# One chunk's band attention moves from TensorE to VectorE, idle products fill TensorE's gaps, and the opening gets a written-out order

## The chip, the cores and the metric

The kernel runs on one core of a Trainium2 chip. The metric is the device time of one execution in microseconds (us); smaller is better.

## What is computed

The reference is attention in two resolutions, added up, and a gated network on the result.

```python
q_d, k_d, v_d = (t.reshape(8, 8, 144, 4, 64).mean(axis=3) for t in (q, k, v))
coarse = softmax(q_d @ k_d.T / 8) @ v_d          # 144 x 144 for each of 8 batches and 8 heads
local = softmax(where(|i - j| < 4, q @ k.T / 8, -1e9)) @ v   # 576 positions, a band of 7
x = repeat(coarse, 4) + local                    # as 4608 tokens of 512
xn = x / sqrt(mean(x * x) + 1e-6) * rms_g
g = xn @ w_gate                                  # 512 x 1536
out = (silu(g) * (xn @ w_val)) @ w_out           # 1536 x 512
```

Inputs of attention are 32-bit floats; the weights come as 64-bit floats and are decoded on the chip into a high and a low fp32r part.

## The kernel before

The 4608 tokens are worked on in 18 chunks of 256. A chunk needs the local attention of its tokens, the coarse attention of the batches that it touches, the norm, and a transposition into `xh` and `xl` (high and low part). Then the class `Forward` runs: `first` (L1259) forms gate and value with 3 products for each of 4 slices of the model dimension, `second` (L1296) multiplies by `w_out` in the same three-product manner. ScalarE does the tanh, VectorE the gating.

The coarse attention of a batch and two heads is a `Coarse`: scores on TensorE (L498), row maxima on VectorE (L507), exponentials on ScalarE (L517), transposes (L526), values (L540). The result goes to DRAM and comes back in the layout of a chunk (`load_up`). For batch 0 the sums over four positions are formed on the chip from raw inputs (`OpeningSums`: one reduction on VectorE for Q and K, L406, and three additions for V, L415); later batches sum in the DMA, with accumulating loads that POOL issues (L356).

The local attention has two forms. `Attention` works on VectorE: a product of Q with a window of seven K rows (L811), a reduction (L815), the softmax, seven products of share and V row, four on ScalarE (L857) and the others on VectorE and POOL (L864), and a reduction (L874), each eight times a chunk. `Early` works on TensorE: scores of 128 tokens against 136 positions with a mask added by a product (L1048, L1050), row maxima (L1063), exponentials (L1074), shares (L1101), transposes (L1108), value products (L1133), with eight small loads a unit for the positions at the unit's edges (L1036), issued by SP, and the coarse part added by a product with a spreading matrix (L1139). Before, chunks 0 and 1 are `Early` (`ON_TENSOR = 2`), the others `Attention`.

The weights come in 20 pieces, by thirds of the network's width. A piece is loaded by SP into one of a few raw buffers (L249), its bits are scaled on ScalarE (L254), extracted on POOL (L264), joined on VectorE (L271), and split into high (ScalarE, L278) and low part (VectorE, L283 and L285). The place of the second third is also that of chunk 0's and 1's raw inputs and band scores, so that it can only be written when these are done with.

What sets the order: up to the planned time of chunk 3 a planner in the kernel's Python, `Plan`, writes each engine's list by hand. A step is a `task` with an engine (or several to choose from), a cost in us, a due time, the tasks that it waits for and the buffers that it takes. At each turn the planner takes the engine that can start first, and on it, of the tasks that could start within 0.15 us of the first, the one with the smallest due. Each engine then runs its list strictly in order. Due times are formulas: `due` for the chunks (48, 107, 158, then 56 apart), `T - 88 + 7 * n` for a chunk's loads and so on. From chunk 3's network on (`FIRST = 3`) a loop emits chunk c's network with the attention of chunk c + 1 between its steps, and the tile scheduler sets the order.

## Time and profile before

| | us |
|---|---|
| median of 3 runs | 1131.25 |
| lowest and highest | 1128.24, 1132.88 |
| the profiled execution | 1137.31 |
| its span, first to last instruction | 1135.5 |

The profiled execution is 6 us longer than the median; 1.8 us of its time lie outside the span. In the profile, PE is TensorE's products, PEld its weight loads, DVE VectorE, ACT ScalarE, POOL GpSimd, and SP the engine that issues most DMAs; SPq, ACTq and POOLq are DMA issues in these queues. A row of the busy time by stage has the stretch in us from the span's start, its length, for each engine the busy time and the number of instructions, the granted clock, the DMA engines' busy share and GB/s. A row of the chain of waits has start, length, and what ran. A row of a group has the line, engine, operation, tiles and shapes, count, then busy us and mean ns, then idle us before the group and what ended it. A line number is that of the kernel before.

### The profile page before, as it was taken

How to read it: one execution, taken by the hardware profiler on the slowest of the kernel's cores; microseconds unless marked ns; L12 is line 12 of the kernel's file. 1: busy time of each engine (PE TensorE's matmuls, PEld its weight loads, DVE VectorE, ACT ScalarE, POOL GpSimd, SP SyncE). 2: the span in 40 equal slices, each digit the busy share in tenths (PEclk: the TensorE clock that was granted, in tenths of full speed). 3: DMA queues.
4: the chain of work that ended last, by engine and by line, in shares of the span. 5: the costliest groups of instructions: out<-in, count | busy, mean ns of one | idle time of the engine just before them, and what ended most of it. 6: DMA issues, size and time to landing. Idle time of an engine off the chain costs nothing.

```text
span 1135.5 us, 21446 instructions
## 1 busy us (share of the span) xinstructions
PE 1083.9 (95%) x7878; PEld 987.3 (87%) x7878; DVE 900.8 (79%) x1519; ACT 597.8 (53%) x2033; POOL 142.2 (13%) x178
## 2 busy tenths in 40 slices
PE   4699969989999999999999999999999999999997
PEld 3567869869999999999999999999999999999997
DVE  5365987869997979797979797979797989887321
ACT  3465547455646555555555555555555473736111
POOL 4242313332111010101010101010000000000000
PEclk9999989989999999999999999999999999999999
DMA  6755644636264344434343435343131313220000
GB/s 161 272 209 142 179 121 110 127 85 151 67 154 91 109 95 120 85 109 94 109 96 105 99 95 109 103 102 98 43 99 43 103 45 101 69 58 19 1 20 19
DMA packets 79619, 114.07 MB, mean 100 GB/s; under 512 B 32666, under 2 KB 41114, under 8 KB 79514
## 3 DMA queue, kind: packets, MB, share of 16 engines
q1 hardware_dynamic: 50026, 89.52, 25.8%
q0 software_dynamic: 10080, 18.59, 10.5%
q10 hardware_dynamic: 19408, 4.60, 1.9%
q8 instruction: 62, 1.02, 0.4%
q14 instruction: 43, 0.35, 0.1%
HBM read 100.86 MB, written 11.80 MB: 99 GB/s over the span
## 4 chain that ended last, share of the span: by engine, by line
PE 88%; DMA 5%; DVE 2%; ACT 2%; SPq 1%; issue 1%; POOL 0%; ACTq 0%; DVEq 0%; POOLq 0%
PE ps_h L1259 50%; PE ps_o L1296 25%; PE ps_a L540 3%; PE ps_a L498 2%; PE ps_a L526 2%; PE ps_a L926 1%; DMA wo<-in_w_val_dram 1%; PE ps_o L1133 1%; SPq L1036 1%; PE ps_h L1050 1%; DMA w<-in_v_pad_dram 1%; DMA w<-in_v_sum_dram 1%; PE ps_a L1133 1%; DMA q_t<-in_q_band_dram 1%; PE ps_a L1108 0%
## 5 line engine op out<-in xcount | busy, mean ns | idle before, releaser
L1259 PE MATMUL ps_h<-xh,w 128*128 128x256 f32 x3456 | 635.5, 281 | 10.7 <-ACT w L278 6.4
L1259 PEld LDWEIGHTS ps_h<-xh,w 128*128 128x128 f32 x3456 | 540.3, 189 | 22.7 <-ACT w L278 6.8
L1259 PE MATMUL ps_h<-xl,w 128*128 128x256 f32 x1728 | 483.5, 280 | 0.0
L1296 PE MATMUL ps_o<-wo,hs 128*128 128x512 f32 x1296 | 333.5, 399 | 1.7 <-POOL hs L1283 1.6
L1259 PEld LDWEIGHTS ps_h<-xl,w 128*128 128x128 f32 x1728 | 327.2, 189 | 6.5 <-issue 1.7
L857 ACT ACTIVATE prod<-kv,sc 128x64 f32<-128x64 f32 x1024 | 263.7, 407 | 30.4 <-DVE sc L848 19.8
L1296 PEld LDWEIGHTS ps_o<-wo,hs 128*128 128x128 f32 x1296 | 233.4, 189 | 46.4 <-POOL hs L1283 2.7
L874 DVE TENSOR_REDUCE x_t<-prod 128x128 f32<-128x896 f32 x128 | 135.0, 1078 | 47.4 <-PE ps_a L926 41.3
L1266 ACT ACTIVATE sil<-ps_h 128x512 f32<-128x512 f32 x108 | 64.5, 597 | 168.3 <-PE ps_h L1259 159.7
L1280 ACT ACTIVATE hs<-sil 128x512 fp32r<-128x512 f32 x108 | 68.2, 631 | 155.0 <-DVE sil L1274 134.2
L811 DVE TENSOR_TENSOR prod<-q_t,kv 128x896 f32<-128x896 f32 x128 | 140.0, 1099 | 0.5
L815 DVE TENSOR_REDUCE sc<-prod 128x14 f32<-128x896 f32 x128 | 136.7, 1076 | 0.5
L1269 DVE SCALAR_TENSOR_TENSOR sil<-sil,ps_h 128x512 f32<-128x512 f32 x108 | 73.5, 681 | 50.1 <-ACT sil L1266 49.8
L864 DVE TENSOR_TENSOR prod<-sc,kv 128x384 f32<-128x384 f32 (+1 forms) x128 | 103.6, 865 | 0.2
L1274 DVE SCALAR_TENSOR_TENSOR sil<-sil,ps_h 128x512 f32<-128x512 f32 x108 | 74.4, 690 | 30.5 <-PE ps_h L1259 30.3
L356 POOL DMA_DIRECT2D qk<-in_qk_sum_dram x42 | 37.7, 899 | 419.1 <-DMA qk<-in_qk_sum_dram 320.2
L1283 DVE TENSOR_TENSOR hs<-sil,hs 128x512 fp32r<-128x512 f32 x100 | 68.7, 687 | 18.9 <-ACT hs L1280 18.7
L897 ACT ACTIVATE up_t<-x_t 128x128 f32<-128x128 f32 x128 | 39.3, 307 | 44.0 <-DVE x_t L887 39.3
L517 ACT ACTIVATE a_g<-ps_a,m_g 72x144 f32<-72x144 f32 x128 | 46.4, 370 | 15.1 <-DVE m_e L1067 8.3
L605 ACT COPY a_g<-ps_a 72x288 f32<-72x288 f32 x63 | 22.8, 400 | 45.5 <-PE ps_a L526 45.3
L356 POOL DMA_DIRECT2D vs<-in_v_sum_dram x42 | 38.5, 916 | 53.3 <-DMA vs<-in_v_sum_dram 46.4
L540 PEld LDWEIGHTS ps_a<-vs,a_g 72*72 72x72 f32 x512 | 41.8, 159 | 1.3 <-ACT w L1074 0.5
(142 smaller groups left out, 806.9 us busy)
## 6 DMA issues: line engine op xcount, KB each, us to landing
kv<-in_k_pad_dram SPq DMA_DIRECT2D x56, 320.0 KB
kv<-in_v_pad_dram SPq DMA_DIRECT2D x56, 320.0 KB
qk<-in_qk_sum_dram POOLq DMA_DIRECT2D x42, 288.0 KB, 4.5
out_dram<-o_sb SPq DMA_DIRECT2D x96, 72.0 KB
q_t<-in_q_band_dram SPq DMA_DIRECT2D x170, 36.0 KB
vs<-in_v_sum_dram POOLq DMA_DIRECT2D x42, 144.0 KB, 4.4
w<-in_w_gate_dram SPq DMA_DIRECT2D x8, 512.0 KB
w<-in_w_val_dram SPq DMA_DIRECT2D x8, 512.0 KB
```

Of the source, the lines that this page charges most:

```text
L356: nc.gpsimd.dma_start(out=t, in_=(qk_sum, v_sum)[i][self.b, j, :, self.half], accum_op=ALU.add)
L540: nc.tensor.matmul(out=op[:, par, c], lhsT=at[:, kc, c * HALF:(c + 1) * HALF], rhs=self.sums.vs[:, 2 * (self.hp % 2) + par, kc], start=(kc ...
L811: nc.vector.tensor_tensor(out=pr, in0=bcast(q[:, s0:s0 + 2], 2, NO), in1=window(k, s0), op=ALU.mult)
L815: nc.vector.tensor_reduce(out=self.sc[:, j, par, s0:s0 + 2], in_=self.pr[i], axis=AX.X, op=ALU.add,)
L857: nc.scalar.activation(out=self.pr[i][:, o, s], in_=self.v[j, par][:, s0 + s + o], func=AF.Copy, scale=p[:, s, o:o + 1],)
L864: (nc.vector if engine == "DVE" else nc.gpsimd).tensor_tensor(out=self.pr[i][:, a:b], in0=bcast(p[:, :, a:b].rearrange("p s o -> p o s"), ...
L874: nc.vector.tensor_reduce(out=self.x[j][:, s0:s0 + 2, par], in_=pr.rearrange("p o s d -> p s d o"), axis=AX.X, op=ALU.add,)
L1259: nc.tensor.matmul(out=p[n][:, i], lhsT=wi[:, k], rhs=xi[:, k], start=(m == 0), stop=(m == 3 * KT - 1),)
L1269: nc.vector.scalar_tensor_tensor(out=self.sil[n], in0=self.sil[n], scalar=1.0, in1=self.g[n], op0=ALU.add, op1=ALU.mult,)
L1274: nc.vector.scalar_tensor_tensor(out=self.sil[n], in0=self.sil[n], scalar=0.5, in1=self.v[n], op0=ALU.mult, op1=ALU.mult,)
L1283: (nc.gpsimd if engine == "POOL" else nc.vector).tensor_tensor(out=self.hs[n][:, 1], in0=self.sil[n], in1=self.hs[n][:, 0], op=ALU.subtract,)
L1296: nc.tensor.matmul(out=self.o[j], lhsT=lhs[:, cols], rhs=rhs, start=(f == 0 and m == 0), stop=(f == NF - 1 and m == 2),)
```

## The change

Chunk 1 becomes an `Attention`; only chunk 0 stays `Early`. The edge loads of chunk 0's two units go from SP's queue to ScalarE's, as a step of their own. Q's and K's opening sums are three additions instead of one reduction. The planner remembers how long TensorE would idle before a task (`idle`), and `heat` issues products of zeros, 128 wide in contraction and up to 512 columns, into the tile that the next step will overwrite (or, with `fresh=False`, adds zeros to), to fill three quarters of that time where it is over 0.8 us. The small constant loads go from ScalarE's queue to POOL's, behind the start, and the factor matrix `one_sb` is made before the mask. Due times of all 885 tasks are replaced by a list, `RANK`, in tenths of us; among its entries are the edge loads' 126.0 and 104.1 and the small loads' -34.9. Several costs are set anew (score loads of a chunk from 0.15 to 1.8 on SP, exponentials of a `Coarse` from 0.45 to 1.15, transposes from 0.6 to 0.3). The spreading matrix gets smaller, since it serves chunk 0 alone.

```diff
 EDGE = 2 * FAC
-SPREAD = 13 * GRP
+ON_TENSOR = 1
+SPREAD = P * 2 * ON_TENSOR
...
-ON_TENSOR = 2
...
+WARM_AT = 6.5
+WARM_SHARE = 0.75
+WARM_LEAST = 0.6
...
+RANK = [
+    -75, 138, -204, -69, 5, 293, 598, 570, 624, -446, 135, 157, -220, 196, 176, 99, 98, -73, 176, -28, 415,
...
+    -161, 683, -212, 219, 229, -159, 21, 412, 30, 122, 21, 299, -151, 690, -409, 672, 48, 165, 200, 208, 259,
...
+    3289, 1818, 2617, 3401, 3038, 3492, 3243,
+]
...
     def __init__(self, bufs):
-        self.tasks, self.bufs = [], bufs
+        self.tasks, self.bufs, self.idle = [], bufs, 0.0
...
+        if RANK:
+            by = RANK[len(self.tasks)] / 10 - options[0][2]
+            options = [(e, c, d + by) for e, c, d in options]
...
-                        found.append((max(free[e], t.at, at, floor), t))
+                        found.append((max(free[e], t.at, at, floor), t, max(free[e], at)))
...
+            self.idle = s - max(known, WARM_AT) if e == "PE" else 0.0
...
+    zero_sb = const.tile([P, 16], BF16, name="zero_sb")
...
-    X_DUE = [44.0, 60.0]
+    X_DUE = 44.0
...
-    own_place = [(w1[0], QK), (w1[1], QK), (wo[0], 0), (wo[1], 0)]
+    own_place = [(w1[0], QK), (w1[1], QK)]
...
-            add = task("DVE", 2.5, self.add, at, [self.got], allocs=[self.qk_buf])
-            self.q_got = task("ACT", 1.1, self.order, at - 1, [self.got], allocs=[self.q_buf])
+            add = self.got
+            for j in range(1, FAC):
+                add = task(
+                    "DVE", 0.72, lambda j=j: self.add(j), at, [add], allocs=[self.qk_buf] if j == 1 else [], uses=[self.qk_buf],
+                )
+            self.q_got = task("ACT", 1.0, self.order, at - 1, [self.got], allocs=[self.q_buf])
...
-        def add(self):
-            self.qk = glob.tile([P, 2, 2, SD], FP32, name="qk")
-            nc.vector.tensor_reduce(
-                out=self.qk.rearrange("p t h n -> p (t h n)"),
-                in_=self.raw_qk.rearrange("p j x -> p x j"), axis=AX.X, op=ALU.add,
+        def add(self, j):
+            if j == 1:
+                self.qk = glob.tile([P, 2, 2, SD], FP32, name="qk")
+            qk = self.qk.rearrange("p t h n -> p (t h n)")
+            nc.vector.tensor_tensor(
+                out=qk, in0=self.raw_qk[:, 0] if j == 1 else qk, in1=self.raw_qk[:, j], op=ALU.add,
             )
...
+    made = []
+
+    def heat(out, fresh=True):
+
+        n, plan.idle = plan.idle * WARM_SHARE, 0.0
+        cols = 1
+        for d in out.shape[1:]:
+            cols *= d
+        if len(out.shape) > 2:
+            out = out.rearrange({3: "p a b -> p (a b)", 4: "p a b c -> p (a b c)"}[len(out.shape)])
+        cols = min(cols, 4 * P) // P * P
+        for _ in range(int(n * 2400 / cols) if n > WARM_LEAST and made else 0):
+            nc.tensor.matmul(
+                out=out[:, :cols], lhsT=one_sb[:, :out.shape[0]], rhs=bcast(zero_sb, 1, cols // zero_sb.shape[1]), start=fresh, stop=fresh,
+                skip_group_check=not fresh,
             )
...
-                    "ACT", 0.45, lambda par=par: self.powers(par), at, [scale], allocs=[a[par]], uses=[s[par], m, z],
+                    "ACT", 1.15, lambda par=par: self.powers(par), at, [scale], allocs=[a[par]], uses=[s[par], m, z],
...
-                turn = task("PE", 0.6, lambda par=par: self.turn(par), at - TAIL, [exps[par]], allocs=[t[par]], uses=[a[par]])
+                turn = task("PE", 0.3, lambda par=par: self.turn(par), at - TAIL, [exps[par]], allocs=[t[par]], uses=[a[par]])
...
-            values = self.valued = task("PE", 1.3, self.values, at - TAIL, [*copies, *sm.ready_vs], allocs=[o], uses=[*a, sm.vs_buf])
+            values = self.valued = task("PE", 1.15, self.values, at - TAIL, [*copies, *sm.ready_vs], allocs=[o], uses=[*a, sm.vs_buf])
...
+            heat(self.s[0])
...
-                    "SP", 0.15, lambda jp=jp: self.load_score(*jp), T - 88 + 7 * n, allocs=k_bufs[jp],
+                    "SP", 1.8, lambda jp=jp: self.load_score(*jp), T - 88 + 7 * n, allocs=k_bufs[jp],
...
-                    "SP", 0.1, lambda jp=jp: self.load_value(*jp), T - 55 + 7 * n, allocs=[v_bufs[jp]],
+                    "SP", 0.35, lambda jp=jp: self.load_value(*jp), T - 55 + 7 * n, allocs=[v_bufs[jp]],
...
-                load = task("ACT", 0.12, lambda j=j: self.load_up(j), T - 30, up_ready, allocs=[ups[j]], lag=2.5)
+                load = task("ACT", 1.2, lambda j=j: self.load_up(j), T - 30, up_ready, allocs=[ups[j]], lag=2.5)
...
+            heat(tp)
...
-                v_got = task("SP", 0.9, lambda u=u: self.load_values(u), -90 + 12 * u, [clear], uses=[ve], dma=0.5 * MB)
+                v_got = task("SP", 0.4, lambda u=u: self.load_values(u), -90 + 12 * u, dma=0.5 * MB)
+                e_got = task("ACT", 2.8, lambda u=u: self.load_edges(u), -60, [clear], uses=[ve], lag=2.5)
...
-                value = task("PE", 1.75, lambda u=u: self.value(u), at - TAIL, [*parts, v_got], allocs=[y], uses=[*prs, ve])
+                value = task("PE", 2.7, lambda u=u: self.value(u), at - TAIL, [*parts, v_got, e_got], allocs=[y], uses=[*prs, ve])
...
+        def load_edges(self, u):
+            t = HALO + P * u
             first, step = (t - FAC, FAC * (NEAR_K - 1)) if u else (P + HALO, FAC)
             for h in range(H):
                 src = bass.AP(
                     tensor=v_pad.tensor, offset=v_pad.offset + (h * SP + first) * D, ap=[[step * D, 2], [D, FAC], [1, D]],
                 )
-                nc.sync.dma_start(out=self.ve[u][h * EDGE:(h + 1) * EDGE, h * D:(h + 1) * D], in_=src)
+                nc.scalar.dma_start(out=self.ve[u][h * EDGE:(h + 1) * EDGE, h * D:(h + 1) * D], in_=src)
...
+            heat(s)
...
+            heat(y)
...
+            heat(y, fresh=False)
...
-                    lhsT=spread_sb[0][:, GRP + FAC * k:GRP + FAC * k + P], rhs=whole_og["tile"][:, :, :, c],
+                    lhsT=spread_sb[0][:, FAC * k:FAC * k + P], rhs=whole_og["tile"][:, :, :, c],
...
-            if u % 2 == 0:
+            if not hasattr(self, "ss"):
...
+            heat(tp)
...
+                heat(p[n])
...
+            heat(self.o[0], fresh=f == 0)
...
-            "SP", 0.1, lambda: fetch(spot[0].raw_place(spot[1]) if spot else spots[n]), at - 15 - 15 * (fg == 0), allocs=[raw],
+            "SP", 0.35 * m, lambda: fetch(spot[0].raw_place(spot[1]) if spot else spots[n]), at - 15 - 15 * (fg == 0), allocs=[raw],
...
-        bits = task("POOL", (0.93, 1.75)[m - 1], lambda: last_bits("POOL"), at, [got], uses=[raw])
+        bits = task("POOL", (0.75, 1.35)[m - 1], lambda: last_bits("POOL"), at, [got], uses=[raw])
...
-    nc.gpsimd.memset(min_sb, 3e38)
-    for e, at, side in ((0, 0, 0), (1, P - KT, 1), (2, P // 2 - KT, 1), (2, P // 2, 0)):
-        nc.scalar.dma_start(out=min_sb[at:at + KT, e], in_=band_min[(P - KT) * side:(P - KT) * side + KT, side])
-    nc.scalar.dma_start(out=g_sb, in_=rms_g)
-    nc.scalar.dma_start(out=same_sb, in_=same_tok)
+    nc.vector.memset(zero_sb, -1e4)
+    nc.scalar.activation(out=zero_sb, in_=zero_sb, func=AF.Exp)
...
+
+    def make_one():
+        nc.gpsimd.tensor_scalar(out=one_sb, in0=ident_sb, scalar1=2.0 ** 33, scalar2=None, op0=ALU.mult)
+        made.append(one_sb)
...
-        nc.gpsimd.tensor_scalar(out=one_sb, in0=ident_sb, scalar1=2.0 ** 33, scalar2=None, op0=ALU.mult)
...
-        t = first_room(wo[0], A_N + DM, SPREAD)[:HALF]
+        t = first_room(wo[0], 0, SPREAD)[:HALF]
...
-        nc.gpsimd.memset(t, 0.0)
...
-            out=t[:, GRP:GRP + FAC * HALF].rearrange("p (n j) -> p n j", j=FAC), in_=bcast(ident_sb[:HALF, :HALF], 2, FAC),
+            out=t.rearrange("p (n j) -> p n j", j=FAC), in_=bcast(ident_sb[:HALF, :SPREAD // FAC], 2, FAC),
...
+    def load_small():
+        nc.gpsimd.memset(min_sb, 3e38)
+        for e, at, side in ((0, 0, 0), (1, P - KT, 1), (2, P // 2 - KT, 1), (2, P // 2, 0)):
+            nc.gpsimd.dma_start(out=min_sb[at:at + KT, e], in_=band_min[(P - KT) * side:(P - KT) * side + KT, side])
+        nc.gpsimd.dma_start(out=g_sb, in_=rms_g)
+        nc.gpsimd.dma_start(out=same_sb, in_=same_tok)
+
+    small = task("POOL", 6.5, load_small, -40, not_before=2.5, lag=3.0)
+    one_got = task("POOL", 0.6, make_one, -70, not_before=4.5)
...
-        task("POOL", 2.0, make_near, -60, not_before=2.5, allocs=[buf("sil"), buf("sil")]),
+        task("POOL", 1.5, make_near, -60, [one_got], allocs=[buf("sil"), buf("sil")]),
...
-        Early(0).plan(X_DUE[0], (ps_h, "ps_h"), (ps_o, "ps_o")),
-        Early(1).plan(X_DUE[1], (ps_h, "ps_h"), (ps_a, "ps_a")),
+        Early(0).plan(X_DUE, (ps_h, "ps_h"), (ps_o, "ps_o")),
+        Attention(1).plan(),
...
-    atts += [Attention(c).plan() for c in range(ON_TENSOR, FIRST + 1)]
+    atts += [Attention(c).plan() for c in range(2, FIRST + 1)]
...
-    atts[1].turns[0].after += fetched
+    for t in fetched:
+        atts[1].turns[0].after.append(t)
...
```

29 lines of the change are left out of this document (17 added, 12 removed), and 44 rows, old and new, of the table RANK.

## The prediction

> **What bounds the kernel now.** I read the page first, then the busy time by stage, the chain of waits, the queues, and VectorE's groups.
>
> ```profile
> span 1135.5 us, 21446 instructions
> PE 1083.9 (95%) x7878; PEld 987.3 (87%) x7878; DVE 900.8 (79%) x1519; ACT 597.8 (53%) x2033; POOL 142.2 (13%) x178
> ```
>
> TensorE sets the pace of the whole, at 95%. The stages show where the other 5% are. I cut them at the starts of the planned chunks, which the chain of waits gives right below.
>
> ```profile
> core 0: us, PE busy (x) PEld busy (x) DVE busy (x) ACT busy (x) POOL busy (x), PEclk, DMA share, GB/s
> 0.00:8.00 8.00, 0.41 (x1) 0.10 (x1) 1.46 (x1) 1.09 (x1) 6.78 (x22) 1.00 0.78 270
> 8.00:41.00 33.00, 15.81 (x78) 11.74 (x78) 15.55 (x28) 11.74 (x39) 6.37 (x6) 1.00 0.53 139
> 41.00:89.00 48.00, 45.05 (x192) 32.81 (x193) 30.82 (x62) 31.70 (x83) 19.33 (x13) 1.00 0.68 252
> 89.00:110.00 21.00, 19.59 (x70) 14.11 (x69) 10.19 (x15) 9.60 (x27) 5.68 (x6) 1.00 0.59 145
> 110.00:171.00 61.00, 50.62 (x356) 45.67 (x356) 55.05 (x79) 30.85 (x50) 15.84 (x16) 0.92 0.54 146
> 171.00:231.00 60.00, 59.46 (x473) 53.93 (x473) 44.88 (x77) 33.91 (x125) 21.77 (x25) 1.00 0.54 128
> 231.00:252.00 21.00, 15.55 (x82) 11.37 (x81) 13.05 (x24) 11.86 (x47) 8.34 (x19) 0.76 0.28 47
> 252.00:306.00 54.00, 54.00 (x423) 50.47 (x423) 50.06 (x81) 32.95 (x124) 10.81 (x22) 1.00 0.43 104
> 306.00:363.00 57.00, 57.00 (x458) 53.31 (x457) 48.86 (x88) 31.62 (x118) 10.38 (x12) 1.00 0.61 132
> 421.00:1135.00 714.00, 708.44 (x5323) 660.24 (x5321) 579.67 (x982) 369.53 (x1308) 31.63 (x36) 1.00 0.30 78
> ```
>
> ```profile
> 89.75 2.56 PE ps_h L1259 x12
> 92.31 5.61 PE ps_a L1133 x18
> 114.15 2.73 PE ps_h L1259 x24
> 116.88 2.98 PE ps_a L1133 x18
> 145.35 6.86 DMA wo<-in_w_val_dram
> 173.79 1.38 PE ps_h L1259 x12
> 226.81 5.42 DMA up_t<-up
> 251.87 4.11 PE ps_h L1259 x36
> 304.80 7.81 PE ps_h L1259 x67
> ```
>
> The first layer (L1259) of chunk 0 starts at about 89, chunk 1 at about 173, chunk 2 at 252, chunk 3 within the last row, at about 306. From there TensorE is full: 57.00 us of 57, later 708.44 of 714. The diff edits nothing that runs there, so the 1135.5 - 306 = 829.5 us behind it stay, and all that is won or lost is when chunk 3 starts. Three chunks take 54 to 60 us each when they are fed (the stages 252 to 306 and 171 to 231), so of the 306 us some 135 are start-up and waiting: up to 89 no layer runs, about 145 to 158 the weight load of 145.35 and its decoding are waited for, and from 231 to 252 the coarse result that is read back at 226.81.
>
> **The change part by part.** *Edge loads.* What keeps the weights away until 34.8 is SP itself:
>
> ```profile
> 2.35 9.99 SPq L1036 DMA_DIRECT2D kv<-in_v_pad_dram  x8
> 13.73 9.41 SPq L1036 DMA_DIRECT2D kv<-in_v_pad_dram  x8
> 23.69 5.24 SPq L1036 DMA_DIRECT2D kv<-in_v_pad_dram  x8
> 29.48 5.24 SPq L1036 DMA_DIRECT2D kv<-in_v_pad_dram  x8
> 34.77 0.40 SPq L249 DMA_DIRECT2D w<-in_w_gate_dram  x1
> 135.02 0.58 SPq L593 DMA_DIRECT2D kv<-in_k_pad_dram  x1
> 135.65 4.03 SPq L799 DMA_DIRECT2D q_t<-in_q_band_dram  x5
> ```
>
> ```profile
> 41.24 1.12 PE L1108 MATMUL ps_a<-ident_sb,w 128*128 128x128 f32 x4 [10.03 <-ACT a_g L605]
> ```
>
> The 32 small issues hold SP for 9.99 + 9.41 + 5.24 + 5.24 = 29.9 us, with V's sums and every weight behind them; the last row shows TensorE 10.03 us idle until the first weights let ScalarE go on. Sixteen issues vanish with chunk 1's early form, sixteen go to ScalarE's queue. SP gets chunk 1's band loads instead: four score loads at 0.58 + 4.03 = 4.6 us and four value loads at about 0.6, 21 us together, which need not go ahead of the first weights. So these can be issued up to 25 us earlier. Then bytes bind: raw sums (4 MB), a third of the weights (6.3 MB) and chunk 1's bands (3.1 MB), estimated from the shapes, take 50 to 54 us at the 252 to 270 GB/s of the loaded stages. On ScalarE sixteen issues cost from 10 us (16 x 5.24 / 8) to 20 (the 9.99 row, twice); behind them are queued the exponentials of the coarse heads and of chunk 0's band, and TensorE's transposes wait for those. I take 8 of it for the path, nearest to the lower row, as some fall where ScalarE is idle (31.70 busy of 48).
>
> *TensorE.* Chunk 1's early form leaves it: its value products alone are the rows of 18, 5.61 and 2.98 us; with the scores and transposes of two units I put it at 25 us, about three times their sum, half before 89 and half in chunk 0's stretch. The idle products are to quicken the rest: twelve products of L1259 took 2.56 us at 89.75, twenty-four took 2.73 at 114.15, so the opening runs at half speed, though the clock column says 1.00 there. Being busy 45.05 us of 48 did not lift it; some 17 us of wide products behind 89 did. Their cost is nothing in a true gap. If the plan's gaps are not gaps, it is up to three quarters of the 29 us that TensorE idles before 110 (110 - 0.41 - 15.81 - 45.05 - 19.59), 22 us. I take 3, since the queue would mostly wait there for others. By the Trainium skill, "TensorE: Matmul & The Clock Gate", Part 1, some 3.4 us of sustained activity bring the full clock; then it would have come long before 89, the idle products would bring nothing, and the first x would come 10 us later than I say below. The trace disagrees with that, by the 45.05 busy us at half speed.
>
> *First x.* Chunk 0's 89, less 10 for the idle stretch, less 12 for half of chunk 1's early form, less 10 for quicker products (a third of the rest), plus 8 for ScalarE's issues and 3 for idle products: about 68. The bytes allow 54.
>
> *POOL* issues six small loads ahead of the mask that the band scores wait for:
>
> ```profile
> L356 POOL DMA_DIRECT2D qk<-in_qk_sum_dram x42 | 37.7, 899 | 419.1 <-DMA qk<-in_qk_sum_dram 320.2
> ```
>
> At 0.9 us each that is 5.4 us later for the mask, or nothing if the scores wait longer for their raw inputs; 2 of it are in the 68.
>
> *VectorE* is the term that decides.
>
> ```profile
> L811 DVE TENSOR_TENSOR prod<-q_t,kv 128x896 f32<-128x896 f32 x24 | 28.1, 1180 | 0.0
> L815 DVE TENSOR_REDUCE sc<-prod 128x14 f32<-128x896 f32 x24 | 25.8, 1078 | 0.2
> L874 DVE TENSOR_REDUCE x_t<-prod 128x128 f32<-128x896 f32 x20 | 21.7, 1083 | 8.6 <-POOL prod L864 3.5 <-PE ps_a L926 2.4 <-ACT prod L857 2.0
> L874 DVE TENSOR_REDUCE x_t<-prod 128x128 f32<-128x896 f32 x20 | 21.7, 1083 | 8.6 <-POOL prod L864 3.5 <-PE ps_a L926 2.4 <-ACT prod L857 2.0
> L1063 DVE TENSOR_REDUCE m_e<-ps_h 128x2 f32<-128x272 f32 x16 | 6.9, 437 | 16.2 <-PE ps_h L1050 16.2
> L1101 DVE TENSOR_TENSOR wo<-wo,z_e 128x512 f32<-128x512 f32 x4 | 2.6, 684 | 0.0
> L406 DVE TENSOR_REDUCE qk<-w 128x576 f32<-128x2304 f32 x2 | 8.4, 4190 | 6.5 <-DMA w<-in_qk_sum_dram 6.5
> L415 DVE TENSOR_TENSOR vs<-vs,w 72x512 f32<-72x512 f32 x2 | 1.4, 689 | 1.3 <-POOL vs L415 1.3
> ```
>
> Up to 306 it was busy 1.46 + 15.55 + 30.82 + 10.19 + 55.05 + 44.88 + 13.05 + 50.06 = 221 us. Of that, chunk 4's was done ahead: 8 of the 24 at L811 and L815, 4 of 20 at L874, 5 of 21 at L864, which is 9.4 + 8.6 + 4.3 + 2.7 = 25. Chunk 3's start needed 196. Added is chunk 1's band: 8 x (1.180 + 1.078 + 0.545 + 1.083) = 31 us, and 4 for its softmax, coarse sum and norm (four wide instructions near L415's 0.689 and some short ones). Removed is its early form: half of L1063 (3.5), L1101 (2.6), and as much again for copies, Newton steps and the rest: 12. The sums by additions take 6 x 0.689 x 576 / 512 = 4.7 for 8.4, so 4 less. New need: 196 + 31 + 4 - 12 - 4 = 215 us.
>
> How densely can that lie? Needed work filled 196 / 298 = 66% of the time from 8 to 306. Before 110 VectorE was at 55% (56.6 of 102), from 110 to 171, where it had work at hand, at 90% (55.05 of 61), from 252 to 306 at 93%. The new order has work at hand sooner, as chunk 1's band needs only loads. I take 60% from 8 to 68, 36 us, and 90% for the other 179, 199 us: chunk 3 starts at 68 + 199 = 267, 39 us earlier. TensorE would allow 68 + 3 x 54 = 230, so VectorE binds. ScalarE (32 of 54 us busy per chunk) takes chunk 1's products without binding.
>
> *Behind chunk 3* the lead of 25 us on chunk 4 may be gone. Then 48.86 us of VectorE work must fit into 57, which it does at 86%; between 0 and 8 us late, and I take 2. Gain: 39 - 2 = 37. The profiled execution (span 1135.5) would come to 1098.5; the median of the runs, 1131.25, to about 1094.
>
> **The rivals.** *VectorE nearly without holes.* If the searched order gives 93% throughout from 8 on (the stage 252 to 306), chunk 3 starts at 8 + 231 = 239, and 67 us are gained: 1064. For it: the work is independent and loads are early. Against: no stage before 110 came near.
>
> *The weights keep chunk 0 long.* The load at 145.35 waited for a raw buffer to be decoded. If chunk 0 still ends at 171 and only the wait from 231 to 252 goes, the gain is 21: 1110. For it: decoding stays the same work on ScalarE, POOL and VectorE, now beside chunk 1's band. Against: the first weights come 25 us sooner.
>
> *The idle products don't lift the clock,* so that the change doesn't do what it says: first x 10 us later, and the idle products take twice their gaps' share, 5 more: gain 22, 1109. For it: 45.05 us of narrow products didn't lift it. Against: they are wide, as those behind 89 were.
>
> *VectorE as hole-ridden as before.* Chunk 1's band now depends on VectorE, and each engine takes its list strictly in order; if waits on ScalarE's edge loads and on decoded weights leave the fill at 66%, chunk 3 starts at 8 + 215 / 0.66 = 334, 28 us later: 1159. It turns at 215 / 298 = 72%. For it: VectorE gets 20 us more, in the stretch from 110 to 171 where it was at 90% already. Against: half of the holes lay before 89, behind SP.
>
> **How the numbers follow.** The forecast (gain 25 to 50) 0.46; dense 0.16; weights 0.12; clock 0.10; hole-ridden, or anything on that side, 0.11; within 0.5% of no change 0.05, a fill near 72%. 0.5% is about what a measurement of this kernel can tell from no change. Faster: 0.46 + 0.16 + 0.12 + 0.10 = 0.84. The range leaves out the slower side and the ends of the others: from the dense case's 1064 to 1126, a fill of 74%.
>
> **What would show it.** Right: SP's first weight issue before 12 us; L1259 first at 60 to 75; its products 0.114 us apart from the start; no L406 reduction; chunk 3's start at 250 to 280 with VectorE above 85% from 70 on; chunk periods behind it unchanged. Wrong: ScalarE's queue waiting on edge loads; twelve products of L1259 still taking 2.5 us; a wait on a weight load past 120; VectorE under 75% before chunk 3.

## The result, and the profile after

The changed kernel takes 1122.72 us (median of 6 runs, 1120.92 to 1124.66) beside 1131.06 us for the kernel before (6 runs on the same chip, 1128.24 to 1134.02). The ratio is 0.9928, 95% interval 0.9911 to 0.9946: 6 to 10 us faster, where 37 were forecast. The profiled execution has 1121.49 us. That of before lay 6 us above its median, so the two traces differ by 16 us, the medians by 8: about half of what the traces show between before and after belongs to that one execution and not to the change.

The page of the kernel after, its span and the row of busy times:

```profile
span 1119.7 us, 21609 instructions
PE 1074.0 (96%) x7900; PEld 975.3 (87%) x7900; DVE 921.8 (82%) x1528; ACT 604.8 (54%) x2070; POOL 170.5 (15%) x207
```

VectorE has 21 us more than before (921.8 for 900.8), TensorE 10 less (1074.0 for 1083.9), idle products included. The work moved as the diff says. Next the busy time by stage, cut at the starts of the first x (101), chunk 1 (160), chunk 2 (231) and chunk 3 (290):

```profile
core 0: us, PE busy (x) PEld busy (x) DVE busy (x) ACT busy (x) POOL busy (x), PEclk, DMA share, GB/s
0.00:8.00 8.00, 1.75 (x9) 1.51 (x10) 1.41 (x3) 1.50 (x2) 6.96 (x19) 1.00 0.66 216
8.00:41.00 33.00, 21.01 (x110) 14.84 (x108) 24.91 (x41) 14.16 (x49) 16.16 (x16) 0.65 0.90 288
41.00:83.00 42.00, 36.21 (x172) 25.98 (x172) 36.60 (x46) 28.76 (x54) 17.92 (x13) 0.54 0.75 257
83.00:101.00 18.00, 14.99 (x70) 6.91 (x68) 15.56 (x28) 9.67 (x15) 7.03 (x7) 1.00 0.85 221
101.00:160.00 59.00, 54.96 (x405) 50.34 (x407) 56.42 (x76) 39.72 (x118) 30.00 (x37) 1.00 0.48 126
160.00:231.00 71.00, 65.33 (x528) 58.76 (x525) 56.52 (x104) 42.50 (x162) 28.85 (x41) 0.98 0.61 134
231.00:290.00 59.00, 57.88 (x443) 52.56 (x441) 48.05 (x79) 33.11 (x119) 19.16 (x26) 1.00 0.44 106
```

Read the DVE column down to 160, then the PE column. VectorE is dense early: 24.91 of 33 from 8 on, where it had 15.55 before. From 101 to 160 it is full, 56.42 of 59 (96%). From 160 to 290 it has 25 us of holes, and now TensorE is full: 65.33 + 57.88 = 123.2 of 130. A table of the chunks' starts says the same; each is the time of the 1st, 289th, 577th and 865th product of the first layer in the trace (a chunk has 288):

| | chunk 0 | chunk 1 | chunk 2 | chunk 3 | span less chunk 3's start |
|---|---|---|---|---|---|
| before | 89.4 | 173.6 | 251.7 | 305.9 | 829.6 |
| after | 100.5 | 160.4 | 231.2 | 289.5 | 830.2 |

Everything behind chunk 3's start is unchanged, as forecast. The first x comes 11 us later, not 21 earlier; chunk 0's network is done in 50 us (its last first-layer product at 150.3) where it had taken 82 (171.0), and that more than pays for it. What releases the first x, from the chain of waits of the kernel after (start, length, what):

```profile
13.12 0.76 SPq L307
...
22.73 6.54 SPq L307
29.31 8.41 DMA wo<-in_w_out_dram
37.77 1.43 POOL w L322
...
53.52 5.61 PE ps_o L1225 x18
...
75.55 1.91 PE ps_a L623 x16
...
82.57 1.02 PE ps_o L1232 x2
...
90.30 6.02 DMA wo<-in_w_val_dram
96.50 2.08 POOL wo L322
98.61 1.23 DVE wo L329
99.84 1.20 DVE xl L1277 x2
```

SP's first weight issue is at 13.12 instead of 34.77, as promised by the moved edge loads. But between it and the first x stand the coarse values of heads 2 and 3 (L623 at 75.55), their spreading (L1232), and then weights of the later thirds, whose decoding (L322, L329) the list puts ahead of chunk 0's last step L1277.

### The profile page after: what moved, and what is told of

It is laid out like the page before. It is cut to its first block, busy times and chain, and to the rows that moved or that the text cites. A ratio compares the mean times of both kernels' runs of the same rounds, so it can differ in the third digit from the quotient of the medians.

```text
span 1119.7 us, 21609 instructions
## 1 busy us (share of the span) xinstructions
PE 1074.0 (96%) x7900; PEld 975.3 (87%) x7900; DVE 921.8 (82%) x1528; ACT 604.8 (54%) x2070; POOL 170.5 (15%) x207
## 4 chain that ended last, share of the span: by engine, by line
PE 78%; DMA 6%; DVE 6%; ACT 4%; SPq 3%; POOL 2%; issue 1%; ACTq 1%; DVEq 0%; POOLq 0%
PE ps_h L1354 47%; PE ps_o L1392 23%; PE ps_a L623 2%; ACT prod L940 2%; PE ps_a L579 2%; PE ps_a L1010 1%; SPq L882 1%; DMA wo<-in_w_val_dram 1%; DVE prod L894 1%; PE ps_a L608 1%; DMA kv<-in_k_pad_dram 1%; DMA q_t<-in_q_band_dram 1%; DVE sc L898 1%; SPq L307 1%; DMA wo<-in_w_out_dram 1%
## 5 line engine op out<-in xcount | busy, mean ns | idle before, releaser
L1354 PE MATMUL ps_h<-xh,w 128*128 128x256 f32 x3456 | 630.0, 280 | 3.5 <-DVE sil L1364 2.2
L1354 PEld LDWEIGHTS ps_h<-xh,w 128*128 128x128 f32 x3456 | 537.3, 188 | 14.7 <-DVE sil L1364 3.1
L1354 PE MATMUL ps_h<-xl,w 128*128 128x256 f32 x1728 | 482.0, 279 | 0.1
L1392 PE MATMUL ps_o<-wo,hs 128*128 128x512 f32 x1296 | 331.9, 398 | 0.0
L1354 PEld LDWEIGHTS ps_h<-xl,w 128*128 128x128 f32 x1728 | 325.2, 188 | 6.6 <-issue 1.7
L940 ACT ACTIVATE prod<-kv,sc 128x64 f32<-128x64 f32 x1088 | 280.9, 408 | 35.3 <-DVE sc L931 21.1
L1392 PEld LDWEIGHTS ps_o<-wo,hs 128*128 128x128 f32 x1296 | 233.2, 189 | 44.3 <-DVE prod L894 1.7
L957 DVE TENSOR_REDUCE x_t<-prod 128x128 f32<-128x896 f32 x136 | 143.4, 1078 | 48.3 <-PE ps_a L1010 41.4
L894 DVE TENSOR_TENSOR prod<-q_t,kv 128x896 f32<-128x896 f32 x136 | 147.7, 1092 | 6.9 <-DMA q_t<-in_q_band_dram 5.6
L898 DVE TENSOR_REDUCE sc<-prod 128x14 f32<-128x896 f32 x136 | 144.8, 1074 | 0.5
L947 DVE TENSOR_TENSOR prod<-sc,kv 128x384 f32<-128x384 f32 (+1 forms) x136 | 112.4, 878 | 0.3 <-DMA kv<-in_v_pad_dram 0.2
L1378 DVE TENSOR_TENSOR hs<-sil,hs 128x512 fp32r<-128x512 f32 x96 | 65.7, 684 | 18.1 <-ACT hs L1375 18.1
L980 ACT ACTIVATE up_t<-x_t 128x128 f32<-128x128 f32 x136 | 41.9, 308 | 43.8 <-DVE x_t L970 37.1
L598 ACT ACTIVATE a_g<-ps_a,m_g 72x144 f32<-72x144 f32 x128 | 46.4, 370 | 10.6 <-DVE m_g L593 9.9
L623 PEld LDWEIGHTS ps_a<-vs,a_g 72*72 72x72 f32 x512 | 41.2, 157 | 2.6 <-ACT prod L688 1.2
```

What stands on the lines that cost most here:

```text
L894: nc.vector.tensor_tensor(out=pr, in0=bcast(q[:, s0:s0 + 2], 2, NO), in1=window(k, s0), op=ALU.mult)
L898: nc.vector.tensor_reduce(out=self.sc[:, j, par, s0:s0 + 2], in_=self.pr[i], axis=AX.X, op=ALU.add,)
L940: nc.scalar.activation(out=self.pr[i][:, o, s], in_=self.v[j, par][:, s0 + s + o], func=AF.Copy, scale=p[:, s, o:o + 1],)
L947: (nc.vector if engine == "DVE" else nc.gpsimd).tensor_tensor(out=self.pr[i][:, a:b], in0=bcast(p[:, :, a:b].rearrange("p s o -> p o s"), ...
L957: nc.vector.tensor_reduce(out=self.x[j][:, s0:s0 + 2, par], in_=pr.rearrange("p o s d -> p s d o"), axis=AX.X, op=ALU.add,)
L1354: nc.tensor.matmul(out=p[n][:, i], lhsT=wi[:, k], rhs=xi[:, k], start=(m == 0), stop=(m == 3 * KT - 1),)
```

## The experiments

Fifteen kernels ran, each beside the kernel before on the same chip. Starts are read as in the table above, each from one profiled execution. How far they can be trusted shows in the kernels after whose edits moved the time by little (e1, e2, e6, e7, e8, e13, e14): chunk 1 starts there at 160.0 to 162.4, chunk 2 at 230.1 to 235.9, chunk 3 at 287.9 to 294.3. Three kernels compute something else than the reference: e7 and e13 leave batch 1's coarse values out of chunk 2, e14 leaves out half of each head's elements in chunk 1's scores.

| run | chunk 0 | chunk 1 | chunk 2 | chunk 3 | median us | ratio to before, 95% interval |
|---|---|---|---|---|---|---|
| after | 100.5 | 160.4 | 231.2 | 289.5 | 1122.72 | 0.9928 [0.9911, 0.9946] |
| e1 Newton steps on VectorE | 99.4 | 162.2 | 230.1 | 287.9 | 1119.29 | 0.9881 [0.985, 0.9912] |
| e2 no idle products | 100.0 | 161.8 | 235.9 | 294.3 | 1123.61 | 0.992 [0.9891, 0.9949] |
| e3 no list | 87.3 | 181.7 | 253.6 | 307.8 | 1144.12 | 1.010 [1.0062, 1.0139] |
| e4 no list, two chunks on TensorE | 107.5 | 198.8 | 267.4 | 325.7 | 1158.61 | 1.0243 [1.0201, 1.0284] |
| e5 before, edges on ScalarE | 109.2 | 198.9 | 267.8 | 321.1 | 1150.73 | 1.0163 [1.0144, 1.0182] |
| e6 edges back on SP | 100.4 | 160.0 | 233.1 | 291.5 | 1125.15 | 0.9942 [0.992, 0.9963] |
| e7 no wait for batch 1 | 99.5 | 162.3 | 230.5 | 293.3 | 1122.5 | 0.9923 [0.9897, 0.9949] |
| e8 one reduction | 100.4 | 161.5 | 233.8 | 292.2 | 1126.14 | 0.9948 [0.993, 0.9965] |
| e9 first x earlier | 93.1 | 161.7 | 234.7 | 293.8 | 1126.82 | 0.9958 [0.9942, 0.9975] |
| e10 more TensorE | 100.2 | 160.9 | 238.5 | 301.2 | 1133.69 | 1.0031 [1.0012, 1.0051] |
| e11 more VectorE | 99.8 | 171.0 | 247.1 | 307.5 | 1137.96 | 1.0065 [1.0044, 1.0086] |
| e12 before, edges on ScalarE later | 110.6 | 193.1 | 251.5 | 309.1 | 1147.65 | 1.0169 [1.0125, 1.0212] |
| e13 e1 and e7 together | 99.2 | 161.8 | 231.5 | 289.8 | 1123.02 | 0.9915 [0.9883, 0.9948] |
| e14 half scores in chunk 1 | 99.3 | 162.4 | 233.3 | 291.9 | 1125.41 | 0.9936 [0.991, 0.9961] |
| e15 e1, edges later | 101.2 | 165.7 | 230.5 | 288.3 | 1118.89 | 0.9875 [0.9844, 0.9906] |

My first theory was the forecast's own reasons with late queues as the disturber; its rivals were a late first x, and VectorE's density.

**The parts of the change: e2, e3, e4.**

```
-WARM_SHARE = 0.75                     (e2)
+WARM_SHARE = 0.0

-RANK = [ ... ]                        (e3, and in e4)
+RANK = []

-ON_TENSOR = 1                         (e4; with the places and due times
+ON_TENSOR = 2                          of the kernel before)
-        Attention(1).plan(),
+        Early(1).plan(X_DUE[1], (ps_h, "ps_h"), (ps_a, "ps_a")),
```

> The changed kernel without any idle product, all else as it is. Theory 'late first x' with the idle products as a cause (they ran 11 us ahead of the first x's transposes, and at half rate at 77 and 80): chunk 0 starts 2 to 6 us earlier and the time falls by 0 to 5 us, 1118 to 1123. Theory 'the clock matters': without them the first products of chunk 0 run at half speed for longer, chunk 0 takes 5 to 10 us more and the time rises to 1127 to 1132. Theory 'density': TensorE doesn't bind before chunk 3, within 2 us, 1121 to 1125.

> The changed kernel with an empty list, so that the due times are the formulas again; chunk 1 is still on VectorE, the edge loads on ScalarE, the idle products in. Theory 'the order earned the gain': chunk 0 starts earlier (near 80) but chunk 1's x later than 160, chunk 3 past 306, time 1135 to 1150. Theory 'the moves earned it' (SP freed, chunk 1 on VectorE): within 5 us of the changed kernel, 1118 to 1128.

> As e3, and chunk 1 back in its TensorE form: only the edge loads on ScalarE, the idle products, the additions and the new costs are left of the change. Against e3 it gives the price of the move by itself. Theory 'density' (VectorE binds before chunk 3, and the move adds 20 us to it): 10 to 25 us faster than e3. Theory 'queues': within 5 us of e3. My forecast's own reasons (SP freed brings the weights 25 us sooner) want it 15 to 25 us faster than the kernel before, 1106 to 1116; if what SP gives is lost on ScalarE, it is within 6 us of the kernel before.

Without the idle products the time is the same within what the intervals tell, some 4 us. They do lift the clock: here are TensorE's first products of chunk 0 without them, then with them (start, length, three products from row pair to row pair).

```profile
101.06 0.63 PE L1354 MATMUL ps_h<-xh,w 128*128 128x256 f32 x2
101.49 0.41 PE L1354 MATMUL ps_h<-xl,w 128*128 128x256 f32 x1
101.70 0.63 PE L1354 MATMUL ps_h<-xh,w 128*128 128x256 f32 x2
```

```profile
84.27 11.00 PE L494 MATMUL ps_a<-zero_sb,one_sb 128*128 128x512 bf16 x50
...
101.31 0.40 PE L1354 MATMUL ps_h<-xh,w 128*128 128x256 f32 x2
101.55 0.28 PE L1354 MATMUL ps_h<-xl,w 128*128 128x256 f32 x1
101.67 0.40 PE L1354 MATMUL ps_h<-xh,w 128*128 128x256 f32 x2
```

Three products take 0.64 us without them (101.06 to 101.70) and 0.36 with them (101.31 to 101.67). But the slow rate ends by itself at 105.75, within 6 us of dense products, so some 26 products too slow by 0.1 us each, 2.6 us, are what it costs there. The list is worth more than the whole gain: without it the kernel is 1% slower than before, some 20 us behind the kernel after, although its first x comes at 87.3.

What the move of chunk 1 earns by itself isn't shown. e3 has chunk 1's band on VectorE and is 14.5 us faster than e4, but e4 also has 32 edge loads in ScalarE's queue where e3 has 16. The stage from 8 to 41, e4 first, then e3:

```profile
8.00:41.00 33.00, 5.73 (x37) 4.15 (x37) 6.18 (x11) 0.00 (x0) 13.59 (x19) 0.67 0.90 286
8.00:41.00 33.00, 21.37 (x130) 15.86 (x131) 15.61 (x32) 9.72 (x37) 13.24 (x18) 0.76 0.96 306
```

In e4 ScalarE computes nothing there (0.00) and copies Q at 41.69, in e3 at 22.30; the next group shows what such a delay can cost. e4 against before, 27 us slower, holds the same 32 issues.

**The edge loads: e5, e12, e6.**

```
-  v_got = task("SP", 0.9, ... self.load_values(u), -90 + 12 * u, [clear], uses=[ve], ...)     (before)
+  v_got = task("SP", 0.4, ... self.load_values(u), -90 + 12 * u, ...)
+  e_got = task("ACT", 2.8, ... self.load_edges(u), -60, [clear], uses=[ve], lag=2.5)          (e5)
+  e_got = task("ACT", 7.0, ... self.load_edges(u), 20 + 8 * u, [clear], uses=[ve], lag=2.5)   (e12)
-                nc.sync.dma_start(out=self.ve[u][...], in_=src)
+                nc.scalar.dma_start(out=self.ve[u][...], in_=src)

-  e_got = task("ACT", 2.8, ... self.load_edges(u), ...)                                       (after)
+  e_got = task("SP", 2.8, ... self.load_edges(u), ...)                                        (e6)
```

> The kernel before with one part of the change: its 32 small edge loads are issued by ScalarE as steps of their own instead of by SP, so that SP has the raw sums, V and the weights to itself; two chunks stay on TensorE, and nothing else is changed. My forecast's reason: the first weight issue comes some 20 us earlier (34.8 to about 15), chunk 0 starts 10 us or more earlier than its 89 and the time falls by 10 us or more, to 1121 or less. 'Queues': 32 issues at 0.7 to 0.9 us hold ScalarE for some 25 us in the stretch in which the exponentials run, so the first x doesn't come earlier: chunk 0 at 85 to 100, time 1126 to 1140. 'Late first x': the time follows chunk 0's start, whatever that is, one for one.

> The kernel before with its 32 edge loads on ScalarE as in the kernel with the edges moved alone, but due 20 to 50 us later, so that the copies of Q and the first exponentials go ahead of them in ScalarE's queue. If the loss of the earlier run (19 us) was that ScalarE stood behind the edge loads until 45 us, it goes, and what is left is what SP's freedom is worth: by my forecast's reason chunk 0 starts 10 us or more earlier than 89 and the time is 1121 or less; 'queues' says that the 20 us of issues fall on the path elsewhere: 1128 to 1138.

> The kernel after with the sixteen edge loads issued by SP again, as one step for each block at the place that the list gives the step. 'Queues': ScalarE is free of some 15 us of issues ahead of the first copies and exponentials, SP's weights come later by as much; as the weights were ready some 35 us before the first x in the kernel after, the first x (100.5) comes 3 to 10 us earlier and the time falls by 2 to 8 us, to 1115 to 1121. My forecast's reason: SP bound, so the weights come later again and the time rises by 5 us or more, above 1127. 'Late first x': the gain or loss is that of chunk 0's start.

In the order of before, the move makes the kernel 1.6% slower. The chain of e5 shows why; the rows between the first two are of the same form:

```profile
32.98 0.62 ACTq L1040
...
44.31 0.62 ACTq L1040
45.08 1.18 issue
46.26 1.96 ACT hs L402
```

```profile
ACT L402 <- DMA kv<-in_v_pad_dram: 45.0, 1, 45.0
```

The first weight issue did come at 17.9 instead of 34.8, but ScalarE's copy of Q, on which all band scores on TensorE hang, stood behind 32 issues until 46.26, where it had run at 8.2 before. With the loads due later (e12) ScalarE still issued from 7.6 to 93.7 and the first x came at 110.6. So SP gained 17 us at its first weight, and ScalarE lost 38 at its copy of Q. In the list's order the same move is worth nothing either way: e6 issues the edge loads from SP, its copy of Q runs at 6.6 instead of 14.9, its first weight issue at 15.2 instead of 13.1, and the first x stays at 100.4. The time is 2 us above the kernel after, which the intervals can't tell from no difference.

**The sums: e8.**

```
+            if j == 1:
+                nc.vector.tensor_reduce(out=qk, in_=self.raw_qk.rearrange("p j x -> p x j"), axis=AX.X, op=ALU.add)
```

> The kernel after with the four raw parts of Q's and K's sums added by one reduction per half again, in the place of the first of the three additions. The reduction took 4.19 us in the kernel before, three additions at 0.689 x 576 / 512 take 2.3: VectorE works 3.7 us more near 10 to 25 us. All theories: chunk 3 and the time 0 to 4 us later, 1123 to 1127; more only if the steps behind the first half's sums run behind the first x, which 'late first x' would show as chunk 0 starting later by the same.

One reduction took 4.22 us, an addition 0.75 to 0.80, so three save 1.9 us per half, 3.7 in all. The ratio rose by 0.2% (2 us); the intervals allow this as well as nothing.

**The first x: e9.** The ranks of 68 steps up to chunk 0's input were lowered by 5 to 36 us, more than the expectation says, and those of 86 decoding steps raised by 5.

> The kernel after with the ranks of the list shifted for some steps: the coarse heads 2 and 3, chunk 0's norm and input and V's sums of the opening 2 to 20 us earlier, the weight decoding 5 us later; the work is the same. Chunk 0's first layer should start some 5 us earlier than 100.5, chunk 0's end stays near 150. 'TensorE full behind the first x' (178.5 us of TensorE work lie between the first x at 100.5 and chunk 3's start at 289.5, only 10.5 us are idle): chunk 3 starts 3 to 6 us earlier, 1117 to 1120. 'VectorE's work' (217 us of it have to be done ahead of chunk 3, in whatever order): no gain, 1121 to 1126. 'The list is a searched optimum': any shift costs, 1125 or more.

The first x came 7.4 us earlier, at 93.1, and all of it was lost at once: chunk 1 starts at 161.7. The stage from 101 to 160 of e9:

```profile
101.00:160.00 59.00, 49.87 (x339) 45.05 (x338) 51.32 (x72) 38.94 (x114) 31.29 (x37) 0.94 0.54 145
```

TensorE has 49.87 for 54.96: it began sooner and then waited, longest, 5.0 us, for VectorE's gating. The chain of waits of e9 from 96 on holds weights now decoded later (their load from 100.30 for 7.02 us, their extraction on POOL at 108.09); that these are the reason is read from the chain, and no run tested it. "Late first x" falls, and with it "TensorE full behind the first x" for chunk 0.

**Prices by stage: e10 and e11.** Both add a known load at the same 72 places, 24 in each of chunks 0 to 2.

```
+            for _ in range(2 * (self.att.c < FIRST)):                              (e10)
+                nc.tensor.matmul(out=p[n][:, i], lhsT=one_sb, rhs=bcast(zero_sb, 1, C // 16), start=True, stop=True)

+            if self.att.c < FIRST:                                                 (e11)
+                for _ in range(2):
+                    nc.vector.tensor_tensor(out=spare, in0=ident_sb[:, :48], in1=ident_sb[:, :48], op=ALU.add)
```

> The kernel after with two products of zeros (128 x 256) ahead of each of the 72 groups of twelve first-layer products of chunks 0 to 2: 144 x 0.11 = 16 us more TensorE work between the first x and chunk 3's start, and nothing else. It prices TensorE's time in that stretch. 'TensorE full behind the first x': 10 to 16 us later, 1133 to 1139. 'VectorE's work': 0 to 5 us later, 1122 to 1128. 'Queues': in between, 5 to 10 us.

> The kernel after with two small additions on VectorE (128 x 48) at each of the same 72 places: 144 x 0.1 to 0.17 = 14 to 24 us more VectorE work in the same stretch, and nothing else. It prices VectorE's time there. 'VectorE's work': later by nearly all of it, 12 us or more, 1135 or more. 'TensorE full behind the first x': 0 to 6 us later, as VectorE has 40 us of holes between 101 and 289, 1122 to 1129.

Neither theory holds for the whole stretch, but by chunks there is an answer. TensorE's addition is 48 x 0.114 = 5.5 us per chunk. VectorE's held the engine for 14.1, 11.3 and 8.3 us (busy time that it added to the engine's list in the trace, by the stretches between the starts). The starts move against the kernel after by:

| | chunk 1 | chunk 2 beyond that | chunk 3 beyond that |
|---|---|---|---|
| e10, 5.5 us of TensorE per chunk | 0.5 | 6.8 | 4.4 |
| e11, 14.1, 11.3, 8.3 us of VectorE | 10.6 | 5.3 | 2.1 |

In chunk 0 a microsecond of TensorE costs a tenth of itself and one of VectorE three quarters; in chunks 1 and 2 TensorE's costs all of itself (11.2 of 11.0), VectorE's 0.5 and then 0.25. These are the stages of e10 from 101 on, to be laid beside those of the kernel after:

```profile
101.00:160.00 59.00, 59.00 (x447) 53.22 (x447) 56.23 (x74) 40.14 (x117) 30.29 (x36) 1.00 0.49 124
160.00:231.00 71.00, 65.44 (x545) 58.65 (x544) 51.76 (x97) 39.98 (x155) 26.86 (x39) 0.99 0.58 129
```

In the first, TensorE's 4 us of holes are filled to 59.00 and VectorE's 56.23 stays: the load fell into the gaps. In the second TensorE did as much as without the load, so the work slid out behind 231. New theory: VectorE sets chunk 1's start, TensorE the two behind it. The single prices are rough, since each rests on differences of starts that vary by 2 to 6 us between kernels of nearly the same time; TensorE's sum over two chunks, 11.2, and VectorE's 10.6 at chunk 1 are clear of that. They also reckon that a late chunk 1 is handed on in full, which e15 below contradicts: its chunk 1 starts 5.3 us later than in the kernel after, its chunk 2 0.7 earlier.

**Work taken away: e1, e7, e13, e14.**

```
-            root = task(newton, ..., lambda: self.root(newton), ...)              (e1, e13)
+            root = task(newton, ..., lambda: self.root("DVE"), ...)

-                stored[b, hp] for b in {b for j in range(2) for _, b, _, _ in spans(2 * c + j)} for hp in range(KT)
+                stored[b, hp] for b in ({0} if c == 2 else {...}) for hp in range(KT)     (e7, e13)
-                src = up_dram[b].rearrange("k t n d -> n k t d")
+                src = up_dram[0 if self.c == 2 else b].rearrange("k t n d -> n k t d")

+            d = D // 2 if self.c == 1 else D                                      (e14)
+            nc.vector.tensor_tensor(out=pr[..., :d], ...)     and the sums over d elements
```

> The changed kernel, with the Newton steps of chunks 1 to 3 on VectorE in the places where POOL had them. In the changed kernel chunk 2's norm stands behind POOL: at 216 to 222 POOL waits for a landing to issue an accumulating load, and the Newton steps are queued behind it (222.78 to 224.24); chunk 1's and 3's take 4 us on POOL. Theory 'queues' (the missing 22 us before chunk 3 are waits between the engines' lists): chunk 2 starts 6 to 8 us earlier, chunk 3 5 to 10 earlier, the time falls to 1113 to 1118. Theory 'late first x' (the 32 us that chunk 0 starts later than forecast are handed on): no change, 1121 to 1124. Theory 'density' (VectorE binds, and every us added to it counts): 3 to 6 us slower, 1126 to 1129.

> The kernel after, in which chunk 2 adds the coarse values of batch 0 in place of those of batch 1, so that its squares, norm and input no longer wait for batch 1's coarse attention, which still runs. It prices the late tail of chunk 2's input. 'Queues': the raw sums of batch 1, gathered by accumulating loads in POOL's queue, are what make chunk 2 start at 231 with TensorE idle from 214.5: chunk 2 starts 8 to 15 us earlier, chunk 3 at 275 to 283 and the time falls by 7 to 14 us, to 1108 to 1115. 'Density': VectorE's own backlog decides, so chunk 3 moves by 3 us or less and the time stays within 3 us of the kernel after. 'Late first x': no change before chunk 2, and none behind it that the opening did not cause.

> The kernel after with both edits on chunk 2's tail: the Newton steps of the planned chunks on VectorE instead of POOL, and chunk 2 adds batch 0's coarse values in place of batch 1's, so that it doesn't wait for them. Alone the first gave 3 to 5 us, the second nothing (in that run the Newton steps still stood in POOL's queue behind an accumulating load until 217.2). 'Queues, two waits side by side': together they end chunk 2's tail, chunk 2 starts at 220 to 226 instead of 231, and the time falls to 1110 to 1116. 'VectorE up to chunk 1's start, TensorE behind it': TensorE is idle for only some 6 us between chunk 1's start and chunk 2's, so at most that is to be had: chunk 2 at 225 to 230, 1115 to 1119.

> The kernel after, in which chunk 1's band scores are made from half of the 64 elements of each head: the eight products and eight sums (1.18 and 1.08 us in the kernel before) take about half, 9 us less VectorE work ahead of chunk 1's start, and nothing else. 'VectorE up to chunk 1's start, TensorE behind it' (VectorE is busy 95% of 110 to 170): chunk 1 starts 6 to 9 us earlier than 160.4 and chunk 3 and the time follow by 5 to 9 us, to 1114 to 1118. 'TensorE alone, from the first x on': chunk 0's 50 us of TensorE work end near 150 whatever VectorE does, so 0 to 4 us earlier. 'The order is fixed by the list': 0 to 2 us, as VectorE only waits longer at its next step.

e1 gains 0.3% over the kernel after by the medians, 0.5% by the ratios; its interval overlaps that of after by a hair. e7 alone gains nothing. In its trace POOL's queue shows what took the place of the wait:

```profile
211.04 0.85 POOL L414 DMA_DIRECT2D vs<-in_v_sum_dram  x1 [2.50 <-DMA vs<-in_v_sum_dram]
216.35 0.83 POOL L414 DMA_DIRECT2D vs<-in_v_sum_dram  x1 [4.46 <-DMA vs<-in_v_sum_dram]
216.91 0.51 POOL L718 TENSOR_TENSOR newton<-rinv 128x8 f32<-128x8 f32 x1
```

The Newton steps (L718) still start at 216.9, as in the kernel after (217.1): they stand in POOL's queue behind an accumulating load that waits 4.46 us for the one before. They end 4 us sooner (220.5 for 224.4), and chunk 2 still starts at 230.5. That asked for e13, both edits at once, and it gains nothing over either: it has e1's edit and isn't told from the kernel after, so e1's gain is less sure than its own interval says. Its chain ahead of chunk 2:

```profile
210.51 4.76 DMA vs<-in_v_sum_dram
215.27 0.34 issue
215.61 3.27 DMA vs<-in_v_sum_dram
218.88 0.14 issue
219.02 2.15 PE ps_a L623 x16
221.17 4.86 PE ps_o L1392 x12
226.03 0.44 PE ps_a L1010 x4
226.46 2.75 PE ps_o L1392 x12
229.21 0.44 PE ps_a L1010 x4
```

Chunk 2's norm (L997) ran at 216.8 and 219.9 in this run, but its transposes (L1010) come at 226.03 and 229.21: in TensorE's queue they stand behind batch 1's coarse values (L623), which wait for V's sums, and behind 24 products of chunk 1's second layer. In this run the queue of TensorE, not chunk 2's input, sets its start.

e14 refutes my new theory in its simple form. Chunk 1's products took 0.62 us for 1.09 and the sums 0.61 for 1.08, some 7 us less, and nothing came sooner. Two stages of e14:

```profile
8.00:41.00 33.00, 21.57 (x112) 15.60 (x111) 21.54 (x41) 14.16 (x49) 16.89 (x16) 0.64 0.91 290
...
101.00:160.00 59.00, 52.31 (x390) 47.90 (x389) 55.98 (x71) 38.16 (x114) 27.78 (x36) 1.00 0.48 121
```

From 8 to 41 VectorE has 21.54 us for 24.91, but all sixteen shortened instructions lie ahead of the first x, where VectorE isn't full (71.5 of 93 us from 8 to 101); from 101 to 160 it still has 55.98 of 59. So the theory stands only for work that lies behind the first x: e11 and the 96% speak for it there, and no run took such work away.

**A better version: e15.** e1, and the edge loads not planned ahead of 8 us.

```
-  e_got = task("ACT", 2.8, ..., lag=2.5)
+  e_got = task("ACT", 2.8, ..., lag=2.5, not_before=8.0)
-            root = task(newton, ..., lambda: self.root(newton), ...)
+            root = task(newton, ..., lambda: self.root("DVE"), ...)
```

> A candidate: the kernel after with the planned chunks' Newton steps on VectorE, and the edge loads not ahead of 8 us in the plan, so that ScalarE's first copy of Q and the first exponentials are not queued behind thirteen of them. 'Queues': the first x 3 to 8 us earlier than 100.5 and 2 to 6 us more than the 4 of the Newton steps alone: 1113 to 1117. 'VectorE up to chunk 1's start, TensorE behind it': no more than the Newton steps alone, 1118 to 1120, since an earlier first x only stretches chunk 0.

1118.89 us is the fastest time of all, 0.3% under the kernel after by the medians, 0.5% by the ratios, and no different from e1 alone. The first x did not move (101.2). The second edit did half of what it was for: the first copy of Q runs at 6.64 instead of 14.90, but all sixteen issues now stand ahead of the second, which waits 17.4 us for them and runs at 25.17 instead of 18.42. So nothing here shows a gain by the edge loads, and edge loads behind both copies were not run in the list's order. Its stages from 101 on:

```profile
160.00:231.00 71.00, 69.51 (x554) 62.35 (x553) 60.93 (x119) 44.13 (x165) 23.91 (x28) 0.98 0.60 131
231.00:290.00 59.00, 58.02 (x440) 52.63 (x440) 49.56 (x90) 34.05 (x124) 12.62 (x15) 1.00 0.48 113
```

TensorE has 127.5 of 130 us here (123.2 in the kernel after): behind chunk 1's start there is next to nothing left to gain by waits.

## Why the prediction was wrong, step by step

The step that failed is *first x*, "about 68", and with it the sum "chunk 3 starts at 68 + 199". It came at 100.5; the 189 us behind it were even fewer than the 199. The list accounts for 13 of these 32 us at most, since without it the first x is at 87.3. For the other 19 the runs name no single cause: in that order ScalarE's copy of Q runs at 22.30, behind sixteen edge issues, for 8.2 before, and no run took these away there.

- *Bytes and SP.* Nearly right: the first weight issue is at 13.12 (said: before 12), and the loads move 288 GB/s from 8 to 41 for 139 before.
- *ScalarE's edge issues, 8 us on the path.* In the kernel after they are what its first copy of Q (L464) waits for, as the issues' own view says:

```profile
  ACT hs L464: 12.2, 1
```

  In the list's order this cost nothing (e6), in the order of before 17 to 19 us, with 32 of them (e12, e5). The size was wrong in both; what counts is who is queued behind, and who waits for that.
- *Ten us for the idle stretch, twelve for half of chunk 1's early form, ten for quicker products.* None of the 32 us came at the first x. The work did leave TensorE, and its longest wait between 8 and 42 fell from 10.03 us to 5.84, but the first x came no sooner for it: the list used the room on VectorE for weights and for all eight of chunk 1's scores, ahead of chunk 0's input. Without the list the first x is at 87.3, with shifted ranks at 93.1, and neither kernel is faster. I had taken the first x as a goal by itself. By e9's chain it is worth something only if the weights are decoded by then.
- *Idle products lift the clock.* They do, and the first products run at full rate, but e2 finds no price for that beyond its intervals. The forecast's rival that they don't lift it was wrong too. Without them the slow rate ends by itself within 6 us of dense products. By the Trainium skill, "TensorE: Matmul & The Clock Gate", Part 1, some 3.4 us of sustained activity do it; the trace of e2 shows 5.8 us of these products (99.95 to 105.75), longer but of that size. The 45 busy us at half rate of the kernel before stay against it, and no run shows why (below). The forecast's "some 17 us of wide products" was a misreading: of the time from 89.4 to 107 in the kernel before, 24 first-layer products took 5 us and L1139's four 3.7; most of the rest was narrow.
- *VectorE.* The need was right: 239.5 us busy by 290, less 22.6 done ahead for chunk 4 (eight scores and sums, two value sums, a softmax), makes 217; 215 were forecast. The idle time was right in sum, 290 - 239.5 = 50.5 us, forecast 267 - 215 = 52, but by luck, as it lay elsewhere: 22.5 us ahead of 101 (32 forecast ahead of the first x) and 28 behind it (20). In this sum the miss of 22.5 us is the 22.6 of chunk 4 that I had struck out as a lost lead. It was not lost, because from 160 on VectorE was no longer what was waited for and filled its holes with chunk 4. A sum of one engine's work over a stretch with two bounds, one behind the other, gives neither.
- *"TensorE would allow 68 + 3 x 54 = 230, so VectorE binds."* This was mis-sized. Behind the first x TensorE was busy 54.96 + 65.33 + 57.88 = 178 us, not 162: by the trace 155 of the network's two layers (L1354 102.9, L1392 51.7), 18.7 of coarse heads (L579, L608, L623) and 5 of norms and transposes. The 54 per chunk came from one short stage of before; a full period has 57. From 100.5 that allows 279; it was 289.5. e10 shows that in chunks 1 and 2 TensorE does bind.
- *The sums* (3.7 us fewer measured, 4 forecast), *the tail* (830.2 for 829.6, chunk periods of 57) and *the range* (1064 to 1126) held, the last at its slow end. Of the rivals none was right: chunk 0 became short (the first x to its last first-layer product took 50 us, not 82), and VectorE's fill of needed work was 217 / 281.5 = 77%, between the forecast and the hole-ridden rival's 66%.

What stays open is whether another order of the same steps brings the first x and the decoding forward together. e9 is one shifted list, not a search.

## What to carry to other kernels

Price an engine by stage: add a small known load to it at the same places in each stage and see how far the next stage's start moves. Here a microsecond of TensorE cost a tenth in one stage and all of itself in the next, while the mean shares (96% and 82%) told nothing of it; taking a wait away (e7, e13) priced nothing, since the next engine in line was as late, and taking work away (e14) priced nothing either, as it lay in another stage. And moving DMA issues to another queue is only as good as what stands behind them there: 32 issues cost 1.6% in one order, 16 nothing in the other.
